# Replanning the DMA queues of a statically ordered attention and Fourier-MLP kernel

## The chip, the cores and the metric

The kernel runs on one core of one Trainium2 chip. The metric is the device time of one execution in microseconds (us); the time of a kernel is the median over its runs. Five engines work side by side on a core: TensorE (PE, with its weight loads as PEld), VectorE (DVE), ScalarE (ACT), GpSimd (POOL) and SyncE (SP). In this kernel DMA transfers are issued by two of them, SP and POOL, which makes two queues.

## The reference

Four batches, eight heads, 768 positions, head size 64; model width 512, MLP width 2048. All tensors are float32.

```python
P = sort_net                                   # (4, 8, 8, 8)
for _ in range(5):                             # Sinkhorn
    P = exp(P - max(P, -1)); P = P / sum(P, -1); P = P / sum(P, -2)
k_sorted = einsum('bhij,bhjcd->bhicd', P, k in 8 blocks of 96)   # v_sorted likewise
scores = 0.125 * q_block @ k_sorted_block.T    # 96 x 96, block by block
x = softmax(scores) @ v_sorted_block           # (4, 768, 512) over all heads
u = x + real(fft(fft(x, axis=1), axis=2))
un = (u - mean(u)) / sqrt(var(u) + 1e-6)
out = u + relu(un @ w_ch1) @ w_ch2
```

## The kernel before

The whole program is a list of steps, each with the engines that may do it, its cost in nanoseconds on each, and the buffers that it reads and writes. `Plan.run` puts the steps in order before anything runs: it keeps a clock for each engine, looks at all steps whose predecessors are placed, and places the one that can start first (among those within 40 ns, the one of highest priority). `Plan.emit` then advances the clocks. What it writes out is a fixed order of instructions for each engine; on the chip an engine takes its instructions in that order and waits at each for its operands. So a cost or a release time in the planner changes no instruction, but it changes where each one stands.

For DMA steps the planner before has two kinds of cost. Bulk loads have `kb`, and share one transfer clock at 0.235 KB per ns with 1800 ns of start. All other transfers have a fixed `hop` after the issue, raised by 1500 ns while that clock is ahead. `rel` is a time before which a step isn't placed. `need` gives a step a priority by due time.

The work of a batch, with the names of steps and lines that come up later:

- Loads. `load_v` (L432, SP, 384 KB each for a pair of heads), `load_kq` (L440, POOL, 192 KB each after the conversion to 16 bit), `weights` (L1097 for `w1`, L1101 for `w2`, POOL, four parts of 512 KB each), `load_const` (L1107, SP: `cse`, `cso`, `cdh`, `cdl`, `negm`, `lm`, `rsel`, `idx`).
- Block sorting. `make_kron` (L473) spreads the Sinkhorn matrix; `v_cast`, `v_sum` (POOL, L459 to L461); `q_mix` (L625), `k_mix` (L642) and its evictions to `kz`; `v_mix` (L596, L598), evicted into `vo`. `v_move` (L608) moves `vo` to the layout `vs`, in twelve transfers of 65 KB a batch; only in batch 0 may POOL issue some of them. `a_out` (L578) and `row_zero` (L586) are small moves of rows.
- Attention. In batches 0 and 1 each head has its maxima (L700, L703), scores again (L716, L719) and the exponential (L724). In batches 2 and 3 the step `turned` does it in the transposed layout: scores (L737), minima (L747), eight exponentials (L742), `es` (L757 or L759), and two DMA transposes `turn_e` on SP (L761) into `eT`. `values` is L783 with the division L789, L790.
- Fourier part. Folds (L807, L812), transforms along the sequence (`dft_s`, L828, L849) and along the width (`dft_d`, L881 to L897), `residual` (L924, L927), `add_res` (POOL, L947, L948), `store_u` (L954), statistics (L965), `normal` (L990, L993), and the transposes of the normed rows: on PE (L1016) or, in batches 2 and 3, mostly by DMA (`turn_u`, L1006).
- MLP. Two groups of 384 rows a batch: 64 matmuls L1044 with the relu L1050, then 48 matmuls L1065, the sum with `u` (L1072), loaded by `load_u` (L1030), and a scattered store on POOL (L1087). The planner puts MLP into gaps of the other work and at the end.

Batch b + 1 is loaded and mixed while batch b is in its attention and Fourier part.

Of the kernel before, what the change touches and what calls it, by code (L numbers as in the profile page):

```python
# [187 lines left out]
class Step:  # L188
    __slots__ = ("name", "b", "on", "fn", "pre", "data", "succ", "wait", "use", "kb", "hop", "prio", "fin", "by", "rel",
                 "extra")  # L190


class Plan:
    LAG, PE_TAIL, MARGIN, NEAR = 45.0, 215.0, 120.0, 40.0
    DMA_START, DMA_RATE, DMA_CROWD = 1800.0, 0.235, 1500

    def __init__(self, engines):
        self.engines, self.rings = engines, {}
        self.wrote, self.read = {}, {}
        self.todo = []  # L200
        self.free = dict.fromkeys(engines, 0.0)
        self.dma = 0.0
        self.began = False
# [5 lines left out]

    def step(self, name, b, on, fn, r=(), w=(), kb=0, hop=0, need=None, prio=None, rel=0.0):  # L210
        s = Step()
        s.name, s.b, s.on, s.fn, s.kb, s.hop, s.rel = name, b, on, fn, kb, hop, rel
# [69 lines left out]
    def start(self, free):  # L282
        for s in self.wrote.values():
            s.fin = free["T"]
        self.free = dict(free)
        self.dma = free["T"] + 1500
        for r in self.rings.values():
            for h in r.held:
                if h is not None:
                    h.free_at = free["T"]  # L290

    def run(self):
# [9 lines left out]
        while ready:  # L302
            found = []
            for s in ready:
# [26 lines left out]
def kernel(  # L331
# [96 lines left out]
    def load_v(b, hp, need):  # L428
        v32[b, hp] = Buf("hr" if 4 * b + hp in (0, 1, 2, 3, 7) else "v32")

        def f(e):
            nc.sync.dma_start(v_view(b, hp), v[b, 2 * hp:2 * hp + 2].rearrange(  # L432
                "h (p g) d -> p h (g d)", g=G))
        step("load_v", b, {"S": 400}, f, w=[v32[b, hp]], kb=393, need=need, rel=18000 if b == 1 else 0.0)

    def load_kq(b, hp, need):
        hs = slice(2 * hp, 2 * hp + 2)
        for d, src, tag in ((k16, k, "k16"), (q16, q, "q16")):
            d[b, hp] = Buf(tag)
            step("load_" + tag, b, {"G": 740}, lambda e, t=d[b, hp], src=src: nc.gpsimd.dma_start(  # L440
                t.t, src[b, hs].rearrange("h (p g) d -> p h (g d)", g=G)),
                w=[d[b, hp]], kb=393, need=need, rel=32000 if b == 1 else 0.0)

# [131 lines left out]
    def a_out(b):  # L575
        def f(e):
            for p, lo, hi, at in ((BLK, 0, 8, 0), (BLK + 1, 0, 7, 1), (BLK + 1, 7, 8, 4)):
                nc.sync.dma_start(xr2[b % 2][p:p + 1, lo:hi].rearrange("o i m -> o (i m)"),  # L578
                                  a16[at:at + hi - lo])
        step("a_out", b, {"S": 2100}, f, r=["a16"], w=[("xa", b % 2)], hop=4500)  # L580

    def row_zero(b):
        def f(e):
            xr = xr2[b % 2]
            for lo, hi, at in ((0, 7, 1), (7, 8, 4)):
                nc.sync.dma_start(xr[BLK + 2:BLK + 3, lo:hi], xr[0:1, at:at + hi - lo])  # L586
        step("row_zero", b, {"S": 1100}, f, r=[("x", b % 2, h, y) for h in range(H) for y in range(2)],
             w=[("x0", b % 2)], hop=4500)

# [15 lines left out]
    def v_move(b, half):  # L605
        for g in range(G):
            def f(e, g=g):
                (nc.gpsimd if e == "G" else nc.sync).dma_start(  # L608
                    vs[2 * (b % 2) + half][16 * g:16 * g + 16].rearrange("c i e -> c (i e)"),
                    vo[half][:, g].rearrange("p h e -> p (h e)"))  # L610
            step("v_move", b, {"S": 600, "G": 560} if b == 0 else {"S": 600}, f,
                 r=[("vo", 4 * half + j) for j in range(4)], w=[("vs", b % 2, half, g)], hop=5500)

    qT = {}

    def q_mix(b, hp):
# [14 lines left out]
        plan.chain(("psQ", b, {"T": 530}, f, [q16[b, hp]], [pQ]),  # L631
                   ("qT", b, {"A": 799, "V": 545}, ev, [pQ], [qT[b, hp]]))

    def k_mix(b, hp, gh):
# [11 lines left out]
        def ev(e, hh):  # L646
# [4 lines left out]
                 SCALE if b < TURN else -SCALE)  # L651
        plan.chain(("psK", b, {"T": 360}, f, [k16[b, hp], (kron[b], hp // 2)], [pK]),
                   *[("kz", b, {"A": 484, "V": 551}, lambda e, hh=hh: ev(e, hh), [pK],
# [74 lines left out]
    def turned(n):  # L728
# [22 lines left out]
        for y in range(2):  # L751
            es = Buf("es")

            def g(e, y=y, es=es):
# [196 lines left out]
    def store_u(b, i, m):  # L951
# [3 lines left out]
            u_dram[b][BLK * t:BLK * t + BLK], us[b, i, m].t[o:o + BLK]),  # L955
            r=[us[b, i, m]], w=[("ud", b, t)], hop=3300)

# [41 lines left out]
    def transpose_u(b, i, m):  # L999
# [5 lines left out]
        if b >= 2 and (i, m) != (0, 1):  # L1005
            step("turn_u", b, {"S": 1250}, lambda e: nc.sync.dma_start(  # L1006
                unT[b, t // 4].t[:, :, BLK * (t % 4):BLK * (t % 4) + BLK],
                un[b, i, m].t[0:BLK], transpose=True),
                r=[un[b, i, m]], w=[(unT[b, t // 4], t % 4)], hop=4000)
            return  # L1010
# [12 lines left out]
    def mlp(b, gr):  # L1023
        hr, ur = {}, {}

        def load_u(t):
# [4 lines left out]
                 r=[("ud", b, j) for j in range(8) if BLK * j < r1 and BLK * j + BLK > r0],  # L1031
                 w=[ur[t]], hop=2800, prio=MLP - 1e8)
        MLP = 1e6 + 1e4 * b
# [43 lines left out]
    def store(b, q_, o, prio):  # L1077
        if (b, q_) == (B - 1, 5):
            for y, (r, n, k0, st) in enumerate((
# [3 lines left out]
                step("store", b, {e_: 400}, lambda e, r=r, n=n, k0=k0, st=st: plan.engines[e].dma_start(  # L1083
                    out[b, k0:k0 + st * (n - 1) + 1:st], o.t[r:r + n]), r=[o], hop=2000, prio=prio)
            return
# [3 lines left out]
            out_offset=bass.IndirectOffsetOnAxis(ap=idx[:, c:c + 1], axis=0),  # L1089
            in_=o.t, in_offset=None), r=[o, "idx"], hop=2500, prio=prio)  # L1090

    def weights(i, need):
        c = i % 4

        def f(e):
# [4 lines left out]
            else:  # L1100
                nc.gpsimd.dma_start(  # L1101
                    w2sb[:, 4 * c:4 * c + 4],
                    moe_w_ch2[DM * c:DM * c + DM].rearrange("(c p) m -> p c m", p=128))
        step("weights", 0, {"G": 770}, f, w=[("w1" if i < 4 else "w2", c)], kb=1048, need=need, rel=45000)

    def load_const(key, need, t, d):
        step("const", 0, {"S": 400}, lambda e: nc.sync.dma_start(t, d.ap()),  # L1107
             w=[key], kb=int(np.prod(t.shape)) * 2 // 1000 + 1, need=need)

# [177 lines left out]
```

## Time and profile before

| | |
|---|---|
| median of three runs | 333.4 us (332.53 to 333.9) |
| profiled execution | 334.52 us |
| its span | 332.4 us |
| granted TensorE clock, mean | 0.979 |
| instructions | 7517 |
| PE busy | 301.2 us (91% of the span) |
| VectorE busy, ScalarE busy | 216.3 us, 213.6 us |
| GpSimd busy | 143.4 us |
| DMA moved | 45.75 MB, 138 GB/s on the mean |
| costliest line on PE | L1044, 512 matmuls, 91.5 us; L1065, 384 matmuls, 89.5 us |

The span runs from the first to the last instruction of the profiled execution; its own time is 2.1 us longer and 1.1 us above the median. A busy PE is modelled from pipelined matmuls, so groups of matmuls overlap by a little in the timeline. In the timeline a line gives start, length, engine, line, operation, operands and the number of instructions merged, and in brackets the idle time of the engine before it and what ended that.

### The profile page before, as it was taken

Reading aid. Unit: us, or ns where it says so; the run is one execution under the profiler, and the core shown is the slowest. Engines: PE = TensorE matmul, PEld = TensorE weight load, DVE = VectorE, ACT = ScalarE, POOL = GpSimd, SP = SyncE. Lnnn points to the kernel's source line nnn. Section 1 sums busy time; section 2 is a strip of 40 time slices with the busy share of each in tenths; the row PEclk is TensorE's granted clock in tenths of the full one; section 3 lists DMA queues with packets and bytes.
Section 4 is the critical chain, followed back from the end, with each engine's and each line's share of the span. In section 5 each row is a group of like instructions: output and inputs, shape, how many; then the busy total and the mean of one; then the engine's idle time right before and its main releaser. Section 6 shows DMA issues by size and latency. Waiting matters only on the chain.

```text
span 332.4 us, 7517 instructions
## 1 busy us (share of the span) xinstructions
PE 301.2 (91%) x2758; PEld 191.9 (58%) x2758; DVE 216.3 (65%) x482; ACT 213.6 (64%) x522; POOL 143.4 (43%) x199
## 2 busy tenths in 40 slices
PE   0998898978999989967999998999999999999993
PEld 0367875746876665545666764566565464554641
DVE  6678796889998999548997899965840502002010
ACT  5564886877798889866985767884276371440710
POOL 8885687778014997323201732310940511202111
PEclk9997998987999999999999999999999999999999
DMA  6999969999607769655425545631651613404112
GB/s 177 216 300 172 164 124 184 233 240 246 174 3 126 137 192 189 188 148 104 109 52 145 146 124 128 170 100 25 172 184 27 184 65 104 130 4 128 63 63 64
DMA packets 53868, 45.75 MB, mean 138 GB/s; under 512 B 23537, under 2 KB 45520, under 8 KB 53832
## 3 DMA queue, kind: packets, MB, share of 16 engines
q1 hardware_dynamic: 38840, 28.31, 32.2%
q0 software_dynamic: 14992, 16.97, 26.7%
q8 instruction: 21, 0.34, 0.5%
q14 instruction: 15, 0.12, 0.1%
HBM read 35.36 MB, written 12.58 MB: 144 GB/s over the span
## 4 chain that ended last, share of the span: by engine, by line
PE 45%; DVE 7%; ACT 5%; issue 3%; DMA 3%; SPq 1%; POOLq 0%; DVEq 0%; ACTq 0%
PE bank L1044 18%; PE bank L1065 18%; ACT sm L742 2%; PE bank L828 1%; DVE es L759 1%; PE bank L783 1%; DMA v<-in_v_dram 1%; DVE mns L747 1%; DVE st L965 1%; PE bank L897 1%; DMA out_dram<-outt,idx_sb 1%; PE bank L737 1%; ACT hr L1050 1%; DMA u_dram<-u 1%; PE bank L596 1%
## 5 line engine op out<-in xcount | busy, mean ns | idle before, releaser
L1044 PE MATMUL bank<-unT,w1sb 128*128 128x384 f16 x512 | 91.5, 329 | 2.4 <-DVE xr L790 2.2
L1065 PE MATMUL bank<-w2sb,hr 128*128 128x512 f16 x384 | 89.5, 379 | 0.1
L1050 ACT ACTIVATE hr<-bank 128x384 f16<-128x384 f32 x128 | 61.7, 492 | 39.5 <-PE bank L1044 38.4
L1044 PEld LDWEIGHTS <-w1sb 128*128 128x128 f16 x512 | 49.1, 99 | 33.5 <-issue 3.3
L1087 POOL DMA_INDIRECT out_dram<-outt,idx_sb x23 | 22.7, 987 | 87.5 <-DVE outt L1072 69.0
L1065 PEld LDWEIGHTS <-hr 128*128 128x128 f16 x384 | 36.5, 98 | 39.5
L1072 DVE SCALAR_TENSOR_TENSOR outt<-ur,bank 128x512 f32<-128x512 f32 x24 | 16.4, 682 | 60.4 <-PE bank L1065 58.0
L742 ACT ACTIVATE sm<-bank,mns 96x96 f32<-96x96 f32 x128 | 31.7, 354 | 6.5 <-DVE mns L747 6.4
L947 POOL TENSOR_TENSOR u<-u,P 96x257 f32<-96x257 f32 (+1 forms) x16 | 11.9, 741 | 39.9 <-issue 15.7
L459 POOL TENSOR_TENSOR v<-v 128x384 f32<-128x384 f32 x11 | 11.0, 1004 | 34.7 <-ACT v L413 22.9
L965 DVE BATCH_NORM_STATS2 st<-u 96x6 f32<-96x512 f32 (+1 forms) x32 | 21.8, 682 | 5.8 <-POOL u L948 5.5
L790 DVE TENSOR_TENSOR xr<-bank,rz 96x512 f16<-96x512 f32 x32 | 22.0, 687 | 1.1
L415 ACT ACTIVATE kz<-bank 64x384 f16<-64x384 f32 x40 | 18.5, 482 | 4.6 <-DVE kz L419 3.8
L783 PE MATMUL bank<-vs,eT 97*96 97x65 f16 x256 | 16.1, 208 | 1.3 <-DVE xr L790 0.5
L807 DVE TENSOR_TENSOR xs<-xr 96x512 f16<-96x512 f16 x32 | 16.9, 540 | 0.3
L783 PEld LDWEIGHTS <-eT 97*96 97x96 f16 x256 | 15.0, 125 | 3.5 <-issue 1.9
L413 ACT COPY u<-bank 96x512 f32<-96x512 f32 (+1 forms) x19 | 10.8, 583 | 8.2 <-issue 3.8
L828 PE MATMUL bank<-cso_sb,xs 96*128 96x384 f16 x64 | 13.1, 326 | 3.2 <-DVE xs L807 3.1
L419 DVE TENSOR_SCALAR kz<-bank 64x384 f16<-64x384 f32 x24 | 12.9, 556 | 4.3 <-ACT kz L415 3.5
L413 ACT CAST W<-bank 128x384 f16<-128x384 f32 (+1 forms) x38 | 12.9, 378 | 4.0 <-PE bank L828 2.5
L993 DVE TENSOR_SCALAR un<-u,mv,rstd 96x512 f16<-96x512 f32 (+1 forms) x19 | 12.0, 641 | 5.1 <-PE bank L1016 5.1
L440 POOL DMA_DIRECT2D k<-in_k_dram x16 | 11.9, 747 | 7.7 <-PE bank L642 5.0
(142 smaller groups left out, 574.6 us busy)
## 6 DMA issues: line engine op xcount, KB each, us to landing
u_dram<-u SPq DMA_DIRECT2D x32, 192.0 KB
ur<-u_dram SPq DMA_DIRECT2D x24, 256.0 KB
v<-in_v_dram SPq DMA_DIRECT2D x11, 384.0 KB
k<-in_k_dram POOLq DMA_DIRECT2D x16, 192.0 KB, 5.7
q<-in_q_dram POOLq DMA_DIRECT2D x16, 192.0 KB, 5.2
vs<-vo SPq DMA_DIRECT2D x42, 65.0 KB
w1sb<-in_moe_w_ch_dram POOLq DMA_DIRECT2D x4, 512.0 KB, 11.2
w2sb<-in_moe_w_ch_dram POOLq DMA_DIRECT2D x4, 512.0 KB, 19.1
```

Source lines behind the costliest of these rows:

```text
L413: nc.scalar.copy(dst, src)
L415: nc.scalar.activation(dst, src, AF.Copy, scale=scale)
L742: nc.scalar.activation(sm.t[:, i], pair(pS, BLK)[:, y, i % 4], AF.Exp, bias=mn.t[:, i:i + 1], scale=-1.0)
L783: nc.tensor.matmul(ps[:, i // 4, i % 4], eT[n].t[0:97, i, :], vs[2 * (b % 2) + h // 4][:, i, (D + 1) * (h % 4):(D + 1) * (h % 4 + 1)])
L790: nc.vector.tensor_tensor(xr2[b % 2][0:BLK, :, D * h:D * (h + 1)].rearrange("p (t j) d -> p t j d", t=2), ps[:, :, :, 0:D], r[:, :, :, Non ...
L807: nc.vector.tensor_tensor(xs[b, hp, par].t, xr[0:BLK, 0:4, ms], xr[0:BLK, 4:8, ms], op=ALU.subtract if par else ALU.add)
L828: nc.tensor.matmul(ps, xs[b, hp, 1].t[:, j, :], cso[:, j, :], start=(j == 0), stop=(j == 3))
L965: nc.vector.bn_stats(st.t[0:n], us[b, i, m].t[0:n])
L1044: nc.tensor.matmul(ps, w1sb[:, mc, 128 * fc:128 * fc + 128], unT[b, gr].t[:, mc, :], start=(mc == 0), stop=(mc == 3))
L1050: nc.scalar.activation(dst, bank(pH, [128, 384]), AF.Relu)
L1065: nc.tensor.matmul(ps, hr[f4].t[:, fc % 4, 128 * t:128 * (t + 1)], w2sb[:, fc, :], start=(fc == 0), stop=(fc == 15))
L1087: step("store", b, {"G": 1020}, lambda e: nc.gpsimd.indirect_dma_start(out=out.rearrange("b s m -> (b s) m"), out_offset=bass.IndirectOffs ...
```

## The change

No operation is added or taken away: the edits are in the planner's account of DMA and in the numbers of the DMA steps.

- `kb` gives way to `work` (time that the transfer takes in its queue), `hop` (time from there to landing), `lanes` (how many of the eight transfers in flight it takes) and `bulk`.
- Each of the two queues, SP and POOL, has a clock of its own. A transfer that starts while the other queue is busy lengthens both, and lands up to 2400 ns later.
- A queue has eight transfers in flight: the ninth is placed when the first has landed.
- A bulk transfer is placed only when the busier queue is less than 800 ns ahead.
- `v_move` may be issued by POOL in every batch, not in batch 0 alone.
- Release times: values of the second batch at 27 us (were 18), its q and k at 29 (were 32), `w1` at 41 and `w2` at 78 (both were 45), inputs of the third batch at 80; `cdh`, `cdl` at 22, `lm`, `rsel`, `idx` at 27 (all had none).
- Planned times: DMA transposes 1250 + 600 + 600 ns (were 1250 + 4000), moves 600 + 450 + 1500 (were 600 + 5500), stores of `u` 350 + 500 + 1300 (were 350 + 3300), loads of `u` 430 + 800 + 2000 (were 430 + 2800); on PE `q_mix` 445 (was 530) and `k_mix` 255 (was 360).

The core of the diff:

```diff
 class Plan:
-    DMA_START, DMA_RATE, DMA_CROWD = 1800.0, 0.235, 1500
+    DMA_AHEAD = 800
...
-        self.dma = 0.0
+        self.dma = {"S": 0.0, "G": 0.0}
+        self.lanes = {"S": [0.0] * 8, "G": [0.0] * 8}
...
-            tail[s] = min(s.on.values()) + (3000.0 if s.kb else s.hop) + max(
+            tail[s] = min(s.on.values()) + (s.work + s.hop + 500.0 if s.hop else 0.0) + max(
...
-        if s.kb:
-            self.dma = max(self.dma, done) + s.kb / self.DMA_RATE
-            done = self.dma + self.DMA_START
         if s.hop:
-            done += s.hop + (self.DMA_CROWD if self.dma > done else 0.0)
+            other = "G" if e == "S" else "S"
+            begin = max(done, self.dma[e])
+            ahead = max(0.0, self.dma[other] - begin)
+            shared = min(s.work, ahead)
+            self.dma[e] = begin + s.work + shared
+            self.dma[other] += shared
+            done = self.dma[e] + s.hop + min(2400.0, ahead)
+            self.lanes[e] = self.lanes[e][s.lanes:] + [done] * s.lanes
...
-                        t = max([at] + [p.fin for p in s.pre if p.by != e or p.kb or p.hop])
+                        t = max([at] + [p.fin for p in s.pre if p.by != e or p.hop])
+                        if s.hop:
+                            t = max(t, self.lanes[e][s.lanes - 1])
+                            if s.bulk:
+                                t = max(t, max(self.dma.values()) - self.DMA_AHEAD)
...
-        step("load_v", b, {"S": 400}, f, w=[v32[b, hp]], kb=393, need=need, rel=18000 if b == 1 else 0.0)
+        step("load_v", b, {"S": 400}, f, w=[v32[b, hp]], work=1250, hop=1450, bulk=True, need=need, rel=80000 if b == 2 else 27000 if b == 1 else 0.0)
...
-                w=[d[b, hp]], kb=393, need=need, rel=32000 if b == 1 else 0.0)
+                w=[d[b, hp]], work=1200, hop=1500, bulk=True, need=need, rel=80000 if b == 2 else 29000 if b == 1 else 0.0)
...
-            step("v_move", b, {"S": 600, "G": 560} if b == 0 else {"S": 600}, f,
-                 r=[("vo", 4 * half + j) for j in range(4)], w=[("vs", b % 2, half, g)], hop=5500)
+            step("v_move", b, {"S": 600, "G": 560}, f,
+                 r=[("vo", 4 * half + j) for j in range(4)], w=[("vs", b % 2, half, g)], work=450, hop=1500)
...
-                r=[es], w=[(et, y)], hop=4000)
+                r=[es], w=[(et, y)], work=600, hop=600)
...
-        step("weights", 0, {"G": 770}, f, w=[("w1" if i < 4 else "w2", c)], kb=1048, need=need, rel=45000)
+        step("weights", 0, {"G": 770}, f, w=[("w1" if i < 4 else "w2", c)], work=3000, hop=1500, bulk=True, need=need, rel=41000 if i < 4 else 78000)
```

The built programs show what the planner makes of it. Both have the same 5261 rows on PE, in another order. Of the twelve moves of a batch, SP issues 6, 6, 5 and 4 (batches 0 to 3; before 6, 12, 12 and 12), POOL the others. On POOL the four loads of `w1` stand apart between value sums and adds, and the four of `w2` behind the adds of batch 0; before, all eight stood in a row. On SP, the values of batch 1 and `lm` come behind the moves of batch 0; before, ahead of them. On PE, the first three pairs' k_mix comes ahead of batch 0's v_mix and the fourth right behind it. VectorE has 492 instructions (482 before) and ScalarE 512 (522).

More of the change, by code (lines that the diff above doesn't have):

```diff
@@ L188 @@
 class Step:
-    __slots__ = ("name", "b", "on", "fn", "pre", "data", "succ", "wait", "use", "kb", "hop", "prio", "fin", "by", "rel",
+    __slots__ = ("name", "b", "on", "fn", "pre", "data", "succ", "wait", "use", "work", "hop", "lanes", "bulk", "prio", "fin", "by", "rel",
                  "extra")
@@ L208, in buf, with step @@
         return b
[L210 removed]
+    def step(self, name, b, on, fn, r=(), w=(), work=0, hop=0, lanes=1, bulk=False, need=None, prio=None,
+             rel=0.0):
         s = Step()
[L212 removed]
+        s.name, s.b, s.on, s.fn, s.work, s.hop, s.rel = name, b, on, fn, work, hop, rel
+        s.lanes, s.bulk = lanes, bulk
         s.data, s.pre, s.succ, s.fin, s.by, s.extra = set(), set(), set(), None, None, []
@@ L285, in start @@
         self.free = dict(free)
-        self.dma = free["T"] + 1500
+        self.dma = dict.fromkeys("SG", 16000)
+        self.lanes = {e: [15000] * 8 for e in "SG"}
         for r in self.rings.values():
@@ L579, in f @@
                                   a16[at:at + hi - lo])
-        step("a_out", b, {"S": 2100}, f, r=["a16"], w=[("xa", b % 2)], hop=4500)
+        step("a_out", b, {"S": 2100}, f, r=["a16"], w=[("xa", b % 2)], work=150, hop=1500, lanes=3)
     def row_zero(b):
@@ L587, in row_zero @@
         step("row_zero", b, {"S": 1100}, f, r=[("x", b % 2, h, y) for h in range(H) for y in range(2)],
-             w=[("x0", b % 2)], hop=4500)
+             w=[("x0", b % 2)], work=100, hop=1100, lanes=2)
     def v_mix(b, h):
@@ L630, in ev @@
                  bank(pQ, [128, G, 128], F16).rearrange("x g (i c) -> x i g c", c=16))
-        plan.chain(("psQ", b, {"T": 530}, f, [q16[b, hp]], [pQ]),
+        plan.chain(("psQ", b, {"T": 445}, f, [q16[b, hp]], [pQ]),
                    ("qT", b, {"A": 799, "V": 545}, ev, [pQ], [qT[b, hp]]))
@@ L651, in ev @@
                  SCALE if b < TURN else -SCALE)
-        plan.chain(("psK", b, {"T": 360}, f, [k16[b, hp], (kron[b], hp // 2)], [pK]),
+        plan.chain(("psK", b, {"T": 255}, f, [k16[b, hp], (kron[b], hp // 2)], [pK]),
                    *[("kz", b, {"A": 484, "V": 551}, lambda e, hh=hh: ev(e, hh), [pK],
@@ L955, in store_u @@
             u_dram[b][BLK * t:BLK * t + BLK], us[b, i, m].t[o:o + BLK]),
-            r=[us[b, i, m]], w=[("ud", b, t)], hop=3300)
+            r=[us[b, i, m]], w=[("ud", b, t)], work=500, hop=1300)
     def stats(b, i):
@@ L1008, in transpose_u @@
                 un[b, i, m].t[0:BLK], transpose=True),
-                r=[un[b, i, m]], w=[(unT[b, t // 4], t % 4)], hop=4000)
+                r=[un[b, i, m]], w=[(unT[b, t // 4], t % 4)], work=600, hop=600)
             return
@@ L1031, in load_u @@
                  r=[("ud", b, j) for j in range(8) if BLK * j < r1 and BLK * j + BLK > r0],
-                 w=[ur[t]], hop=2800, prio=MLP - 1e8)
+                 w=[ur[t]], work=800, hop=2000, prio=MLP - 1e8)
         MLP = 1e6 + 1e4 * b
@@ L1083, in store @@
                 step("store", b, {e_: 400}, lambda e, r=r, n=n, k0=k0, st=st: plan.engines[e].dma_start(
-                    out[b, k0:k0 + st * (n - 1) + 1:st], o.t[r:r + n]), r=[o], hop=2000, prio=prio)
+                    out[b, k0:k0 + st * (n - 1) + 1:st], o.t[r:r + n]), r=[o], work=300, hop=1300, prio=prio)
             return
@@ L1089, in store @@
             out_offset=bass.IndirectOffsetOnAxis(ap=idx[:, c:c + 1], axis=0),
-            in_=o.t, in_offset=None), r=[o, "idx"], hop=2500, prio=prio)
+            in_=o.t, in_offset=None), r=[o, "idx"], work=800, hop=1400, prio=prio)
     def weights(i, need):
@@ L1103, in f @@
                     moe_w_ch2[DM * c:DM * c + DM].rearrange("(c p) m -> p c m", p=128))
-        step("weights", 0, {"G": 770}, f, w=[("w1" if i < 4 else "w2", c)], kb=1048, need=need, rel=45000)
+        step("weights", 0, {"G": 770}, f, w=[("w1" if i < 4 else "w2", c)], work=3000, hop=1500, bulk=True, need=need, rel=41000 if i < 4 else 78000)
     def load_const(key, need, t, d):
         step("const", 0, {"S": 400}, lambda e: nc.sync.dma_start(t, d.ap()),
-             w=[key], kb=int(np.prod(t.shape)) * 2 // 1000 + 1, need=need)
+             w=[key], work=6 * int(np.prod(t.shape)) // 1000 + 50, hop=1500, bulk=t.shape[-1] > 1, need=need,
+             rel=27000 if key in ("lm", "rsel", "idx") else 22000 if key in ("cdh", "cdl") else 0.0)
     rst = const.tile([32, NB], F32, name="rst")
```

## The prediction

> **What bounds the kernel now.** I read the page first, then the busy time by stretches, then TensorE's and VectorE's idle times in the timeline, then the DMA issues. The page's rows of share, clock and DMA:
>
> ```profile
> PE 301.2 (91%) x2758; PEld 191.9 (58%) x2758; DVE 216.3 (65%) x482; ACT 213.6 (64%) x522; POOL 143.4 (43%) x199
> ...
> PEclk9997998987999999999999999999999999999999
> DMA  6999969999607769655425545631651613404112
> ```
>
> PE is busy for 301.2 of 332.4 us. Its first matmul waits 9.08 us for the Sinkhorn steps (L542), its last one ends at 326.9, so 5.5 us of tail follow, and 332.4 - 301.2 - 9.1 - 5.5 = 16.6 us is idle time between matmuls. From 264.6 us on the chain is MLP matmuls alone, back to back (L1044, L1065). PE's work is the same in both kernels, so the change can earn only from these 16.6 us and from a better clock, and can lose wherever PE, which takes its instructions in order, meets a later operand. By stretches of 10 us the idle time lies so: 0.3 in 10 to 20, 6.05 in 20 to 80, 2.4 in 80 to 140, 5.65 in 140 to 160, 2.2 in 160 to 220, 0.3 in 310 to 320 and 0 in between. The four stretches that count, after the column heads:
>
> ```profile
> core 0: us, PE busy (x) PEld busy (x) DVE busy (x) ACT busy (x) POOL busy (x), PEclk, DMA share, GB/s
> 20.00:30.00 10.00, 8.55 (x124) 6.56 (x125) 9.39 (x16) 5.11 (x12) 6.60 (x10) 0.90 1.11 260
> 70.00:80.00 10.00, 8.52 (x69) 5.29 (x67) 9.38 (x18) 6.72 (x16) 8.99 (x13) 0.66 1.21 242
> 140.00:150.00 10.00, 6.84 (x72) 4.68 (x72) 3.38 (x9) 6.73 (x19) 3.13 (x5) 1.00 0.57 148
> 150.00:160.00 10.00, 7.51 (x88) 5.02 (x83) 9.11 (x20) 7.53 (x24) 3.86 (x6) 1.00 0.49 93
> ```
>
> In the first two the DMA share is above 1 and VectorE is nearly full; in 140 to 150 both PE and VectorE starve while DMA is half idle. The timeline there shows why:
>
> ```profile
> 135.62 5.05 SPq L608 DMA_DIRECT2D vs<-vo  x8
> ...
> 142.04 4.87 SPq L761 DMA_TRANSPOSE eT<-es  x2
> ...
> 147.62 0.36 DVE L759 TENSOR_SCALAR es<-sm 96x384 f16<-96x384 f32 x1 [2.51 <-DMA eT<-es]
> ...
> 148.37 0.82 PE L828 MATMUL bank<-cso_sb,xs 96*128 96x384 f16 x4 [2.30 <-DVE xs L807]
> ...
> 150.50 0.56 DVE L417 CAST v<-v 128x768 f16<-128x768 f32 x1 [2.19 <-DMA v<-in_v_dram]
> ```
>
> SP issues the twelve moves of batch 2 (L608) from 132.97 to 141.95, and the transposes and batch 3's value loads stand behind them. VectorE waits 2.51 us for a transpose and 2.19 for a load, and PE waits for VectorE (2.30 us here, 2.15 at 152.81 for L790). The DMA issues and the start:
>
> ```profile
> q<-in_q_dram POOLq DMA_DIRECT2D x16, 192.0 KB, 5.2
> ...
> w1sb<-in_moe_w_ch_dram POOLq DMA_DIRECT2D x4, 512.0 KB, 11.2
> w2sb<-in_moe_w_ch_dram POOLq DMA_DIRECT2D x4, 512.0 KB, 19.1
> ```
> ```profile
> 18.29 0.73 POOL L440 DMA_DIRECT2D q<-in_q_dram  x1
> ...
> 28.87 0.85 PE L625 MATMUL bank<-ident,q 128*64 128x128 f16 x12
> 29.39 0.73 POOL L440 DMA_DIRECT2D k<-in_k_dram  x1 [2.69 <-DMA q<-in_q_dram]
> ...
> 40.87 0.52 PE L700 MATMUL bank<-kz,qT 128*96 128x96 f16 x8 [0.88 <-ACT kz L415]
> ```
>
> The load of q for heads 6 and 7 takes 10.5 us (18.29 to 28.82), since SP queued 2.7 MB of constants and values ahead of it from 14.26 on; the matching k lands at 31.9.
>
> **The sum, part by part.** The span is 332.4, the profiled execution 334.5, the median of the three runs 333.4; the terms are differences on the profile's time and are taken from the median.
>
> *Front, 18 to 45 us.* In the new order `cdh`, `cdl` are behind the short `a_out`, and `lm` and all values of batch 1 behind batch 0's moves; only `cse`, `cso`, `negm` (0.43 MB) are ahead of that q. Loads with little beside them land in 3.4 to 4.3 us (L440 at 108.35 and 105.55), so q is there at about 23 and k, issued when L642 frees its buffer, at about 25. PE's order uses this: all four head pairs' k_mix stands ahead of the scores, where now the fourth (L642) comes at 37.98. Of the 2.3 us of gaps in 20 to 45 I take 1.7 away: the 0.88 at 40.87 wholly, over half of the rest, in which VectorE's maxima bind. Ends: -2.3, and +1.5 as three more kz evictions (0.49 to 0.56 each) get ahead of the first maxima. **-1.7.**
>
> *Weights, 46 to 88 us.* All eight loads leave POOL at 46.2 to 51.4 and occupy the rings until 77.2. Behind them a move takes 6.3 to 8.6 us from issue to landing, against 2.4 to 2.6 at 172 to 177, and as a ninth issue on SP waits until the first of eight has landed (the issue at 72.09 follows a landing at 72.08), the stores and moves stretch from 65 to 83. PE's share of that is the 2.4 us of gaps in 70 to 90, such as 0.56 at 74.86 behind an eviction that waited 0.94 for `u_dram<-u`. The new POOL order has the four w1 loads apart, between sums and adds, and w2 after batch 0's adds, near 80 us. Cover: w1's last part lands at 63.2 now and L1044 starts at 75.5; w2 at 80 + 4 x 3.3 (the pace of L1097) + 5 lands at 98, and L1065 starts at 112.3. I take half of the gaps: **-1.2** (ends -2.4 and 0).
>
> *Moves on two queues.* Now batch 0 has six on each and batches 1 to 3 twelve on SP; then 6, 5 and 4 stay on SP and 6, 7 and 8 go to POOL. An SP issue is 0.59 us on the mean, so for batch 2 SP is free 7 x 0.59 = 4.1 us sooner, which is as much as the two PE gaps of 4.45 us. But one transpose took 3.57 us to issue (142.04) where 1.2 is usual; these 2.37 us were no queue of moves, and I leave them in. 4.45 - 2.37 = **-2.1** (ends -5.65 and 0). On POOL, seven issues of 0.56 stand ahead of value sums and of the loads of k for heads 4 to 7, which the new order puts behind them: 7 x 0.56 + two sums of 1.94 + 0.75 + 4.3 to land = 12.9 us, beside 11.8 us of matmuls between the last L598 of batch 2 and that k_mix. **+0.5** (0 to 1.6).
>
> The Trainium skill, "DMA: Bandwidth & Descriptors", section "Issuing engines are not separate DMA queues", says that a second issuing engine saves the issue time alone, which is usually small beside the transfer. Here it isn't small: 0.59 us of issue each, one after another, against 2.4 to 2.6 us of landing that overlap. By the rule taken strictly the moves would give nothing, and the sum would be 2.1 us worse.
>
> *Tighter plan.* `turn_e` and `turn_u` were planned at 1250 + 4000 ns, now 1250 + 600 + 600. From the semaphore updates of the trace, the 32 transposes of L761 land 2.2 to 6.3 us after issue, median 3.0, mean 3.25; 22 of 32 are later than 2.45 us, 2 later than 5.25. So the reserve that took up lateness is gone. In PE's order the work between a head's scores (L737) and its values (L783) is 12.4 us at the least now; in the new one five of the 16 heads have 8.8 to 10.9. The head's own chain is 0.5 + 0.94 (L747) + 2.0 (eight exponentials) + 0.5 (es) + two issues of 1.2 + 2.3 to land, about 8.6 us. Queued behind a late L783 is all of PE, MLP too. Five heads x 0.8 us (3.25 - 2.45), a third of it met by nothing else: **+1.3** (0 to 16 x 0.8 = 12.8).
>
> *Nothing for the rest.* Ten evictions more go to VectorE and ten fewer to ScalarE; VectorE is at 9.5 to 9.8 of 10 from 80 to 100 and 110 to 130, but PE has MLP to do there (within 1 us). The last groups are as they were: batch 3 is through before MLP needs it in both orders.
>
> Sum: -1.7 - 1.2 - 2.1 + 0.5 + 1.3 = -3.2, so 333.4 - 3.2 = **330.2 us**; the case's own range is 327 to 333.
>
> **Rivals.**
>
> *Tight plan loses (slower).* Place: L783 of batches 2 and 3, 125 to 220 us. Each late transpose holds PE, and the next head's buffers with it. For it: the median is above the planned 2.45. Against it: half of the present lateness stands beside the crowding that goes. Gains of 5.0 less 0.5 are used up when 4.5 of 12.8 us, 35%, is exposed; at 70% it is 333.4 - 4.5 + 9.0 = 337.9 us.
>
> *Hidden anyway (no change).* VectorE, not the queues, sets the pace to 130 us, and the 142 us stall recurs. Then only part of the moves' gain is left: 333.0.
>
> *The clock (faster still).* The granted clock is 0.50 in 28.1 to 31.5, 55.4 to 58.8 and 72.5 to 79.3, with 13.0 us of PE work in it; at full clock that is 6.5 less, of which some 3.4 (the first two, where VectorE isn't full) reach the end: 330.2 - 3.4 = 326.8. The 3.41 us before each had PE busy for only 2.41, 2.57 and 2.15, and the change fills that stage. Against it: 144 to 154 us has 1.92, 2.29 and 1.57 and kept 1.00. The Trainium skill, "TensorE: Matmul & The Clock Gate", section "What's actually happening", ties the half clock to an idle window and full clock to a busy one of some 3.4 us; the trace has the window's length, but not so plain a rule.
>
> That the edit does nothing can be left out: the order of the built program has the moves and weights where it says.
>
> **How the numbers follow.** Forecast 0.48, tight plan 0.25, hidden 0.17, clock 0.10. A measurement here tells about 0.5% (1.7 us; the three runs spread by 1.4). Below 331.7 lie 0.43 of the forecast's chance, the clock's 0.10 and 0.02 of hidden: 0.55. Above 335.1: the tight plan's 0.25 and 0.02 of hidden: 0.27; 0.18 between. The range 325 to 338 leaves out a tenth above and a few hundredths below.
>
> **What would show it.** Right: the load of q at 18 us lands within 5 us; no w2 transfer before 75 us, moves of batch 1 landing in under 4; SP's moves of batch 2 take about 3 us; PE idle in 20 to 90 below 5 us, in 140 to 160 below 3.5. Wrong: PE waiting on L783 or for VectorE behind L783 by more than 4 us in 125 to 220; a wait of L642 for k near 140 us; L1065 waiting for w2.

## The result, and the profile after

| | before | after |
|---|---|---|
| median | 333.2 us (332.5 to 333.9, four runs) | 344.6 us (339.9 to 350.0, four runs) |
| ratio to before | 1 | 1.0284, 95% interval 1.0206 to 1.0362 |
| profiled execution, its span | 334.5 us, 332.4 us | 342.9 us, 340.9 us |
| PE: busy, end of the last matmul | 301.2 us, 326.9 us | 305.3 us, 335.1 us |
| idle between PE's matmuls | 16.6 us | 20.7 us |

By the medians the kernel became 11.4 us slower, where 330.2 us was forecast. Here and below a ratio goes by the faster runs of a kernel alone (two of the four after, 346.3 and 350.0 us, are left out), so that it says 9.5 us where the medians say 11.4. Lines of the changed kernel are 12 higher than before (13 from `weights` on): L761 is L773, L783 is L795, L608 is L620. The page's rows of share, clock and DMA:

```profile
PE 305.3 (90%) x2758; PEld 193.6 (57%) x2758; DVE 220.5 (65%) x492; ACT 211.7 (62%) x513; POOL 154.3 (45%) x219
...
PEclk9999789978999999989999999999999999999998
DMA  7959898997954699993978443641371521503212
```

The busy time in the four stretches that were shown of before, with 130 to 140 and 160 to 170 added:

```profile
core 0: us, PE busy (x) PEld busy (x) DVE busy (x) ACT busy (x) POOL busy (x), PEclk, DMA share, GB/s
20.00:30.00 10.00, 8.96 (x148) 6.53 (x143) 9.94 (x19) 6.39 (x15) 5.15 (x9) 1.00 0.86 178
70.00:80.00 10.00, 8.47 (x71) 6.00 (x71) 8.80 (x19) 6.36 (x13) 8.09 (x12) 0.66 0.77 196
130.00:140.00 10.00, 7.10 (x61) 4.17 (x60) 7.41 (x17) 7.00 (x21) 6.88 (x12) 1.00 1.07 138
140.00:150.00 10.00, 7.75 (x56) 4.64 (x54) 5.25 (x15) 2.95 (x7) 4.96 (x8) 0.83 1.24 200
150.00:160.00 10.00, 9.99 (x134) 6.22 (x132) 9.01 (x20) 8.90 (x25) 3.77 (x6) 1.00 0.25 34
160.00:170.00 10.00, 7.27 (x88) 4.76 (x86) 9.22 (x17) 5.85 (x21) 4.80 (x7) 1.00 1.02 163
```

PE is idle for 1.04 us in 20 to 30 (1.45 before), but over 20 to 45 for as long as before (2.63 and 2.61). The stall of 150 to 160 is gone, 2.25 of 3.16 us are left in 140 to 150, and new gaps stand at 120 to 140 (4.3 us in place of 0.5) and from 160 on. Summed, PE's idle time went from 7.0 to 5.8 us in 20 to 90, from 1.0 to 0.3 in 90 to 120, from 6.2 to 6.6 in 120 to 160, and from 2.2 to 7.7 in 160 to 230. The timeline of the changed kernel at two of these gaps:

```profile
134.89 1.22 SPq L773 DMA_TRANSPOSE eT<-es  x1
...
142.67 0.37 PE L795 MATMUL bank<-vs,eT 97*96 97x65 f16 x4 [2.25 <-DMA eT<-es]
...
168.96 0.52 ACT L769 ACTIVATE es<-sm 96x384 f16<-96x384 f32 x1 [1.49 <-DMA eT<-es]
...
171.60 0.37 PE L795 MATMUL bank<-vs,eT 97*96 97x65 f16 x4 [1.05 <-DMA eT<-es]
171.65 0.36 DVE L771 TENSOR_SCALAR es<-sm 96x384 f16<-96x384 f32 x1 [2.14 <-DMA eT<-es]
```

The transpose issued at 134.89 stands among twelve moves on both queues and lands 7.74 us later; PE has been waiting for it for 2.25. ScalarE and VectorE wait too, since `es`, the source of a transpose, has three buffers. POOL, which the lines below leave out, waits 2.0 us for one. The chain of waits has "DMA eT<-es 5%"; the lines that it names of before have no transpose. The waits that transposes ended in the changed kernel:

```profile
PE bank L795 <- DMA eT<-es: 3.9, 3, 2.3
...
ACT es L769 <- DMA eT<-es: 3.0, 3, 1.5
...
DVE es L771 <- DMA eT<-es: 2.1, 1, 2.1
```

(total, times, longest). Before, PE had none, and the other two 1.9 and 3.3.

### The profile page after: what moved, and what is told of

It is laid out like the page before. It is cut to its first block, busy times and chain, and to the rows that moved or that the text cites. A ratio compares the mean times of both kernels' runs of the same rounds, so it can differ in the third digit from the quotient of the medians.

```text
span 340.9 us, 7526 instructions
## 1 busy us (share of the span) xinstructions
PE 305.3 (90%) x2758; PEld 193.6 (57%) x2758; DVE 220.5 (65%) x492; ACT 211.7 (62%) x513; POOL 154.3 (45%) x219
## 4 chain that ended last, share of the span: by engine, by line
PE 37%; DMA 8%; DVE 8%; ACT 4%; issue 2%; SPq 1%; POOL 0%; POOLq 0%; ACTq 0%; DVEq 0%
PE bank L1056 18%; PE bank L1077 14%; DMA eT<-es 5%; ACT sm L754 2%; DMA ur<-u_dram 1%; DVE st L977 1%; DVE es L771 1%; DVE outt L1084 1%; DVE xr L802 1%; PE bank L909 1%; DVE un L1005 1%; DMA out_dram<-outt,idx_sb 1%; DVE kz L431 1%; DMA xr<-xr 1%; PE bank L795 1%
## 5 line engine op out<-in xcount | busy, mean ns | idle before, releaser
L1077 PE MATMUL bank<-w2sb,hr 128*128 128x512 f16 x384 | 89.5, 379 | 0.5 <-DVE outt L1084 0.4
L1056 PEld LDWEIGHTS <-w1sb 128*128 128x128 f16 x512 | 50.0, 100 | 33.5 <-issue 3.5
L1077 PEld LDWEIGHTS <-hr 128*128 128x128 f16 x384 | 36.4, 98 | 39.7 <-issue 0.8
L1084 DVE SCALAR_TENSOR_TENSOR outt<-ur,bank 128x512 f32<-128x512 f32 x24 | 16.4, 684 | 46.1 <-PE bank L1077 43.9
L1005 DVE TENSOR_SCALAR un<-u,mv,rstd 96x512 f16<-96x512 f32 (+1 forms) x21 | 13.9, 661 | 26.7 <-DMA unT<-un 18.3
L620 POOL DMA_DIRECT2D vs<-vo x27 | 14.5, 545 | 18.4 <-issue 9.0
L795 PE MATMUL bank<-vs,eT 97*96 97x65 f16 x256 | 16.5, 212 | 5.7 <-DMA eT<-es 3.9
L427 ACT ACTIVATE kz<-bank 64x384 f16<-64x384 f32 x36 | 16.9, 486 | 5.4 <-DVE kz L431 4.0
L795 PEld LDWEIGHTS <-eT 97*96 97x96 f16 x256 | 15.3, 129 | 7.9 <-DMA eT<-es 4.3
L425 ACT COPY u<-bank 96x512 f32<-96x512 f32 (+1 forms) x26 | 14.7, 585 | 6.3 <-PE bank L936 4.1
L736 ACT ACTIVATE sm<-bank 96x768 f32<-96x768 f32 x16 | 12.6, 804 | 7.3 <-PE bank L731 6.9
L425 ACT CAST W<-bank 128x384 f16<-128x384 f32 (+1 forms) x39 | 13.6, 393 | 5.5 <-PE bank L840 3.1
L1002 ACT ACTIVATE un<-u,nm,rstd 96x512 f16<-96x512 f32 (+1 forms) x11 | 8.9, 813 | 11.7 <-DMA unT<-un 9.1
L431 DVE TENSOR_SCALAR kz<-bank 64x384 f16<-64x384 f32 x28 | 14.9, 549 | 2.0 <-PE bank L654 1.2
```

Source lines behind the costliest of these rows:

```text
L425: nc.scalar.copy(dst, src)
L431: nc.vector.tensor_scalar(dst, src, scale, None, op0=ALU.mult)
L795: nc.tensor.matmul(ps[:, i // 4, i % 4], eT[n].t[0:97, i, :], vs[2 * (b % 2) + h // 4][:, i, (D + 1) * (h % 4):(D + 1) * (h % 4 + 1)])
L1005: nc.vector.tensor_scalar(o, x, scalar1=mv[b, i].t[0:n, m, 0:1], scalar2=rstd[b, i].t[0:n, m:m + 1], op0=ALU.subtract, op1=ALU.mult)
L1056: nc.tensor.matmul(ps, w1sb[:, mc, 128 * fc:128 * fc + 128], unT[b, gr].t[:, mc, :], start=(mc == 0), stop=(mc == 3))
L1077: nc.tensor.matmul(ps, hr[f4].t[:, fc % 4, 128 * t:128 * (t + 1)], w2sb[:, fc, :], start=(fc == 0), stop=(fc == 15))
```

## The experiments

The theories at the start. T2: transposes planned to land after 2.45 us instead of 5.25 put their readers too close behind them; this planned time, from the start of the issue to the landing, is called the lead below. T1: the order has a hole, as the loads of k for the third batch's head pairs 3 and 4 stand on POOL behind the moves, their key mixing comes at 151 us (before at 108 and 120), and two batches of attention are squeezed into what is left. T3: the moves slow each other on two queues, and the transposes between them. Each run is compared by its ratio to the kernel before, run beside it on the same chip; bracketed pairs are 95% intervals.

**e1_lead.** The changed kernel with the old lead of the transposes:

```diff
# turn_e, and turn_u alike
-                r=[es], w=[(et, y)], work=600, hop=600)
+                r=[es], w=[(et, y)], work=600, hop=3400)
```


> The changed kernel with one part undone: the DMA transposes are planned at 5250 ns from the start of the issue to landing again (1250 + 600 + 3400) instead of 2450. The planner then also puts the key mixing of the third batch's head pairs 3 and 4 (L654 of the changed kernel) ahead of the moves, not 26 us behind them. Theory T1 (the hole: the loads of k for these pairs stand on POOL behind the moves, their scores come 26 us late, and the attention of two batches is squeezed into 150 to 230 us beside loads): about 337 us, gaps of PE in 120 to 230 us down from 14.3 to about 9. Theory T2 (late transposes because of the short lead alone): about 337 us too, but with the waits for eT<-es gone (3.9 us now). Theory T3 (two queues slow each other's moves and the transposes between them): 343 us, no change against the changed kernel.

Measured: 332.6 us, 0.9939 [0.9884, 0.9993]. All of the loss is gone: the ratios differ by 0.0345 of 333 us, 11.5 us, with about 3.2 either way. No engine waits for a transpose any more, and the idle time of PE in 120 to 230 us is 7.0 instead of 14.3. The hole closed too (key mixing of pairs 3 and 4 at 110 and 111 us), so this run alone doesn't tell T1 from T2.

**e2_inputs, e3_moves_sp, e4_no_pacing.** The changed kernel with another part undone, the short lead kept:

```diff
# e2: inputs of the third batch (values, and q and k alike)
-                rel=80000 if b == 2 else 27000 if b == 1 else 0.0)
+                rel=27000 if b == 1 else 0.0)
# e3
-            step("v_move", b, {"S": 600, "G": 560}, f,
+            step("v_move", b, {"S": 600, "G": 560} if b == 0 else {"S": 600}, f,
# e4
-    DMA_AHEAD = 800
+    DMA_AHEAD = 1e9
```


> The changed kernel with one part undone: the inputs of the third batch may be loaded before 80 us again (the release time of 80000 is gone for q, k and v; the second half of the weights keeps its 78 us). Planned order: key mixing of pairs 3 and 4 about half way between the two kernels. T1: about 340 us, half of the hole's price back. T2: 343 us, and more waits for eT<-es than now, since values stand closer behind scores. T3: 343 us.

> The changed kernel with one part undone: the moves of batches two to four are planned and issued on SP alone, as in the kernel before. Planned order: key mixing of pairs 3 and 4 behind the moves still, by about 24 us of matmul work where the kernel before has 17 and the changed one 36. T1: about 341 us. T2: 343 us, no change. T3: about 338 us, moves land in 2.6 us again instead of 5, transposes between them in 3.5 instead of 4.8.

> The changed kernel with one part undone: bulk loads are no longer held back until the busier queue is less than 800 ns ahead. Planned order: key mixing of pairs 3 and 4 stands ahead of the moves, as in the kernel before, and the four parts of w2 and the loads of k and q come in a row. T1: about 337 us. T2: 343 us. T3: 343 us or more, since the loads crowd the moves.

Measured: e2 352.9 us, 1.0595 [1.0515, 1.0675]; e3 347.2 us, 1.0431 [1.0334, 1.0529]; e4 339.2 us, 1.0199 [1.0130, 1.0267]. None of them gets back to before. In e4 the hole is closed (109 and 121 us) and PE is idle for only 2.2 us in 120 to 160, yet for 8.8 in 160 to 230. Its time lies nearer to the 337 us of T1 than to the 343 of T2, and what it gains on the changed kernel (0.0085, with 0.0104 either way) is not clear of noise; but with the hole closed and the lead short it is still 0.0260 slower than e1, 8.7 us with 2.9 either way (pacing differs as well). That speaks against T1 as the main cause. e3 has its moves landing in 3.4 us (median) instead of 5.0 and is no faster: against T3. The waits for `eT<-es` on PE, ScalarE and VectorE together are 9.0 us in the changed kernel, 21.5 in e2, 16.4 in e3, 9.7 in e4 and 0 in e1. e2 and e3 were expected at 343 us by T2 and came out slower. That a short lead makes one pay at once for whatever brings readers nearer or crowds the transposes is argued from this, not shown.

**e5_before_short, e6_lead_u, e7_lead3250, e8_lead7250.** The lead alone: shortened in the kernel before; given back to `turn_u` alone; two other sizes.

```diff
# e5, in the kernel before, turn_e and turn_u
-                r=[es], w=[(et, y)], hop=4000)
+                r=[es], w=[(et, y)], hop=1200)
# e7 (e8: hop=5400), in the changed kernel, turn_e and turn_u; e6: hop=3400 for turn_u alone
-                r=[es], w=[(et, y)], work=600, hop=600)
+                r=[es], w=[(et, y)], work=600, hop=1400)
```


> The kernel before with one part of the change alone: both DMA transposes planned at 2450 ns from the start of the issue to landing (1250 + 1200) instead of 5250; all else as before. T2 (the short lead): waits for eT<-es over PE, ScalarE and VectorE rise from 5.2 us to 9 or more, and the time is 339 to 345 us. Rival T4 (the short lead only hurts together with the new queue costs, pacing and release times): 333 us, within 1%.

> The changed kernel with the lead of 5250 ns given back to turn_u (the transposes of the normed rows) alone; turn_e stays at 2450. T2 in the form that the head's transposes turn_e carry the price: 343 to 346 us, as the changed kernel. If turn_u carries it: about 333 us.

> The changed kernel with both transposes planned at 3250 ns, the mean of the landings measured in the kernel before. If a mean is what a plan needs: 333 us, as with 5250. If the price is the sum of the single latenesses beyond the plan (in the changed kernel 39.9 us beyond 2.45, 24.8 beyond 3.25, 6.0 beyond 5.25, where 12 us came back between the first and the last): about 332.6 + 12.0 x (24.8 - 6.0) / (39.9 - 6.0) = 339 us.

> The changed kernel with both transposes planned at 7250 ns, past nearly all landings. By the lateness that is left beyond 5.25 (0.7 us in the run with 5250) nothing more is to be gained: 332 to 333 us; if distance costs (buffers held longer, values later), 334 to 336 us. Waits for eT<-es stay near 0.

Measured: e5 341.4 us, 1.0272 [1.0225, 1.0318]; e6 346.4 us, 1.0423 [1.0327, 1.0519]; e7 339.0 us, 1.0171 [1.0105, 1.0237]; e8 333.2 us, 1.0008 [0.9969, 1.0047]. e5 settles it: one number in the kernel before, with no other part of the change and no hole in the order (key mixing of pairs 3 and 4 at 110 and 125 us), costs 9 us; T4 falls. e6 puts the price on the heads' transposes, `turn_e`. Under the new account of DMA the hole comes with the short lead (in e6 at 148 us) and goes with the long one (e1, e8), so the 11.5 us hold the hole's price too. By the 8.7 of e4 and the 9.1 of e5 that is up to some 3 us, which lies within the intervals. e7 shows that a mean is not enough: planned at 3.25 us, near the 3.37 of its own landings, it is still about 7 us behind e1. The sum of single latenesses beyond the plan gave 339, and 339.0 came, but so close a hit is luck: the interval is 2.2 us either way, and e4, with 69.4 us of lateness beyond 2.45 in its own trace where the changed kernel has 39.9, is the faster of the two. Past 5.25 us no more is to be had (e8).

**e9_lead_sp, e10_before_two.** The two queues by themselves, with the order on every engine kept; only who issues a move is changed:

```diff
# e9, on top of e1
-                (nc.gpsimd if e == "G" else nc.sync).dma_start(
+                (nc.gpsimd if e == "G" and b == 0 else nc.sync).dma_start(
# e10, in the kernel before
-                (nc.gpsimd if e == "G" else nc.sync).dma_start(
+                (nc.gpsimd if e == "G" or b > 0 and g % 2 else nc.sync).dma_start(
```


> The run with 5250 ns of lead, its order on every engine kept as it is, but each move of batches two to four that stands on POOL is issued by SP at the same place of the order. If two queues are worth the 2.1 us that the prediction gave them: 0.994 + 0.006 = 1.000 of the time of before (about 334.5 us against 332.5). If the second queue only lets the moves slow each other (landing 5.2 us on two queues, 2.6 on one): 0.994 or less.

> The kernel before, its order on every engine kept, but every second move of batches two to four is issued by POOL at the same place of the order. By the prediction's term: 2.1 us faster than before (0.994). If issue time was not what held PE at 140 to 160 us, or if moves on two queues land later: 1.000, with moves of the third batch landing in about 5 us instead of 2.6.

Measured: e9 335.5 us, 1.0046 [1.0000, 1.0092]; e10 339.6 us, 1.0194 [1.0135, 1.0253]. Against e1, taking the second queue away costs 0.0107, or 3.6 us, with about 2.4 either way. It is not lost where the prediction had it: PE's idle time in 120 to 160 is 4.3 us in e9 and 4.7 in e1, while e9 has 2.5 us more in 20 to 120 and 1.5 more in 160 to 230. e10 was expected at 0.994 or 1.000 and is slower, and its timeline says why:

```profile
75.25 0.56 POOL L608 DMA_DIRECT2D vs<-vo  x1 [3.19 <-DMA w2sb<-in_moe_w_ch_dram]
...
79.94 0.73 POOL L440 DMA_DIRECT2D k<-in_k_dram  x1 [4.14 <-DMA w2sb<-in_moe_w_ch_dram]
...
82.14 0.69 DVE L965 BATCH_NORM_STATS2 st<-u 96x6 f32<-96x512 f32 x1 [10.42 <-POOL u L948]
...
85.87 0.80 PE L716 MATMUL bank<-nident_sb,mxs 96*96 96x96 f16 x8 [11.27 <-DVE mxs L703]
```

In the kernel before, the eight loads of weights fill POOL's queue at this place. The moves of the second batch put on it wait for a part of `w2` to land, POOL's adds (L947, L948) wait behind them, VectorE for the adds, and PE stands for 11.27 us. At 120 to 160 us the same edit does what the prediction said: PE is idle there for 2.8 us instead of 6.2. The second queue pays only if the weights are out of its way.

**e11_lead_w2, e12_lead_front.** Two more parts undone on top of e1:

```diff
# e11
-        ... rel=41000 if i < 4 else 78000)
+        ... rel=41000)
# e12: constants; values of the second batch; its q and k
-             rel=27000 if key in ("lm", "rsel", "idx") else 22000 if key in ("cdh", "cdl") else 0.0)
+             rel=0.0)
-                ... rel=80000 if b == 2 else 27000 if b == 1 else 0.0)
+                ... rel=80000 if b == 2 else 18000 if b == 1 else 0.0)
-                ... rel=80000 if b == 2 else 29000 if b == 1 else 0.0)
+                ... rel=80000 if b == 2 else 32000 if b == 1 else 0.0)
```


> The run with 5250 ns of lead, but w2 may be loaded from 41 us as w1, not from 78. By the prediction's term for the weights (1.2 us): 0.994 + 0.004 = 0.998 of before, idle time of PE in 70 to 90 us up again. If pacing and not the release time spreads the loads: 0.994. A re-planned order differs elsewhere too, so that 0.005 either way tells nothing.

> The run with 5250 ns of lead, but with the release times of the constants (cdh, cdl, lm, rsel, idx) taken away and those of the second batch's inputs as before (18 us for values, 32 for q and k). By the prediction's term for the front (1.7 us): 0.994 + 0.005 = 0.999 of before, and the loads of q and k at 18 to 30 us land in 8 to 10 us again. If pacing alone keeps them apart: 0.994, loads landing in about 5.

Measured: e11 333.7 us, 1.0037 [0.9999, 1.0075]; e12 330.2 us, 0.9894 [0.9821, 0.9967]. `w2` at 78 us is worth 0.0098 here, 3.3 us, as far as a re-planned order tells. But PE's idle time in 70 to 90 was not its place: there it is 1.2 us in e11 and 1.8 in e1. The release times of the front are worth nothing; without them the kernel is the fastest so far. The fourth load of q, which took 10.5 us before, lands in 5.5 us in e12 without them, so the rest of the new account keeps the early loads apart.

**e13_four_es, e14_other_leads.** What was left open on the price of the lead: its way to the end, and whether the other shortened transfers have a share.

```diff
# e13, in the changed kernel: es is taken in turn from four buffers, the plan goes by three
-    ring("es", 3, [BLK, 4, 128], F16)
+    ring("es", 3, [BLK, 4, 128], F16)
+    es_more = [const.tile([BLK, 4, 128], F16, name=f"es_more{i}") for i in range(1)]
+    plan.rings["es"].cycle = plan.rings["es"].tiles + es_more
# e14, in the changed kernel: moves hop=5050 (was 1500), a_out 4350 (1500), row_zero 4400 (1100), store_u 2800 (1300)
```


> The changed kernel, its order on every engine kept, with a fourth buffer for es (the source of the transposes), used in turn, so that ScalarE and VectorE wait less for a transpose to be through before they write the next es (3.0 and 2.1 us in the changed kernel). If the lateness reaches the end through these waits: 340 us or less. If it reaches it through PE's own waits at the values (3.9 us) and what is queued behind them: 343 to 345 us.

> The changed kernel with the planned times of the other small transfers as in the kernel before (moves 600 + 5500, a_out and row_zero + 4500, stores of u + 3300), and the transposes still at 2450. If the transposes alone carry the price: 341 to 346 us. If any reserve in the plan does as well: about 334 us.

Measured: e13 343.0 us, 1.0186 [1.0113, 1.0258]; e14 344.8 us, 1.0339 [1.0284, 1.0393]. With four buffers ScalarE and VectorE no longer wait for a transpose, PE's own waits are 5.1 us, and the ratio comes down by 0.0098, with 0.0106 either way. So most of the price goes another way, through PE's waits at the values by T2; up to some 3 us through the other two engines can't be ruled out. The reserve of the other transfers replaces nothing.

**e15_front_lead6250, e16_front_again, e17_front_short.** The kernel of e12 with a lead of 6250 ns (`hop=4400`), as it was, and with the short lead of the change (`hop=600`):

> The run without the release times of the front (lead 5250), with the lead at 6250. No theory asks for a gain: 0.99 of before, within 0.006; tried as the fastest version.

> The same kernel as the run without the release times of the front (lead 5250), on another occasion: 0.989 of before, within 0.006, if it is faster than before; 0.995 to 1.000 if that was chance.

> The run without the release times of the front, with the transposes planned at 2450 again: a third pair that differs in the lead alone. By the other two pairs (+12 us in the changed kernel, +9.3 in the kernel before): 339 to 344 us.

Measured: e15 334.7 us, 1.0005 [0.9951, 1.0058], so a longer lead gains nothing; e16 327.0 us, 0.9883 [0.9820, 0.9947]; e17 341.8 us, 1.0249 [1.0158, 1.0341]. e12 and e16 are one kernel, and both occasions have it about 1.1% faster than before and 4% faster than the changed kernel. e16 and e17 ran on one chip and differ in the lead alone, by 14.8 us (12.2 by the ratios); e17 has the hole too (key mixing of pairs 3 and 4 at 133 and 137 us, in e16 at 105.5 and 107.1). The timeline of e17 shows a long wait for a transpose:

```profile
156.14 10.96 SPq L773 DMA_TRANSPOSE eT<-es  x4
156.35 1.44 POOL L452 DMA_DIRECT2D q<-in_q_dram  x2
...
157.77 1.46 POOL L452 DMA_DIRECT2D k<-in_k_dram  x2
...
165.34 0.53 PE L795 MATMUL bank<-vs,eT 97*96 97x65 f16 x4 [4.14 <-DMA eT<-es]
...
167.81 0.53 PE L795 MATMUL bank<-vs,eT 97*96 97x65 f16 x4 [1.93 <-DMA eT<-es]
```

Three transposes issued beside four loads of q and k (384 KB of source each) land 9.16, 9.50 and 8.28 us after their issue, where the plan said 2.45; PE stands for 4.14 and 1.93 us, and a half clock with 4.6 us of PE's work in it follows from 165.0 on. The two kernels in 160 to 230 us, e17 and then e16:

```profile
160.00:230.00 70.00, 58.33 (x510) 37.62 (x508) 50.82 (x118) 45.68 (x138) 21.57 (x31) 0.93 0.58 113
```
```profile
160.00:230.00 70.00, 67.68 (x582) 42.98 (x581) 61.48 (x141) 52.44 (x161) 29.64 (x43) 1.00 0.52 115
```

Three pairs differ in the lead alone. Idle time is PE's between its matmuls; the clock's loss is half of PE's busy time at a granted clock of 0.5; all from the profiled executions, in us:

| | span | idle 20 to 160 | idle 160 to 230 | clock's loss | waits for eT: PE | ScalarE and VectorE |
|---|---|---|---|---|---|---|
| before | 332.4 | 14.1 | 2.2 | 6.5 | 0 | 5.2 |
| e5, short | 339.3 | 15.6 | 3.3 | 8.2 | 3.1 | 7.4 |
| e1 | 331.3 | 12.0 | 2.3 | 8.4 | 0 | 0 |
| after, short | 340.9 | 12.6 | 7.7 | 8.5 | 3.9 | 5.1 |
| e16 | 323.5 | 9.3 | 2.3 | 1.7 | 0 | 0.3 |
| e17, short | 339.9 | 10.4 | 11.7 | 7.3 | 6.9 | 11.2 |

From e16 to e17 the two columns of idle time give 10.5 us and the clock 5.6, together 16.1 of the 16.4 us between the spans. From e1 to after idle time gives 6.0 of 9.6, and PE is busy 3.7 us longer at about the same loss to the clock; what that is stays open. From before to e5 idle time gives 2.6 and the clock 1.7 of 6.9; the rest, busy time again, stays open too. PE's waits for `eT` are two thirds of the idle time added in the pairs e16, e17 and e1, after (6.9 of 10.5, 3.9 of 6.0), and in the third pair more than all of it (3.1 and 2.6); that the rest stands behind results of VectorE and ScalarE that come later in turn is argued from the order, not shown by a run. Nor does a run have the order of the short lead with its landings on time, so what that order costs by itself is not told apart from the late landings.

## Why the prediction was wrong

*Tighter plan, +1.3: the step that failed.* Mechanism, lines and place were named, as a term and as a rival; the size was off by nine. Measured 11.5 us from e1 to after (3.2 either way, and up to some 3 of it the hole's, which the working didn't have), against ends of 0 and 12.8. Three errors are in the working. First, "five heads x 0.8 us" took the mean landing less the plan. An early landing then pays for a late one, and it shouldn't: the positive parts alone are to be added. From the same trace of before, 22 of 32 transposes are late by 26.6 us together against 2.45, and by 1.3 us against 5.25. A third of 26.6 is 8.9 us, near what e5 measured on this kernel (9.1), but with the third a guess that is luck. Second, the landings were taken as given: against 2.45 us they are 39.9 us late in all in the changed kernel and 27.7 in e1, which differs in the lead alone. In e5, whose order has no hole, they are 24.4 late, no more than before, so the added lateness is not the short plan's alone; that it comes from the crowding behind the hole is argued, not tested. Third, "a third of it met by nothing else" was a guess, and only five heads were counted because the others stood far apart in PE's order. That distance was itself laid out by the short plan. The rival, at 35% exposure or more, had its point of decision right and its chance of 0.25 too low: 11.5 of 12.8 is 90%. What no run settles is how late landings become lost time beyond PE's own waits: e4 has more lateness and less loss.

*Front, -1.7.* The load of q at 18.19 us lands in 3.40 us (10.5 before), as forecast, but the gain isn't there: idle time in 20 to 45 is 2.63 us, as before, in 20 to 90 5.8, not below 5, and the release times behind it, taken away, made e1 0.005 faster on each of two occasions (within the intervals). The load was not what held PE for long.

*Weights, -1.2.* Right in sign, 3.3 us by e11, though the median landing of `w1` and `w2` (7.5 and 8.9 us, 11.2 and 19.1 before) didn't bring the moves of the second batch under 4 us: they land in 6.1 (7.8 before). No wait of L1077 for `w2` appeared. Part of its worth is shown by e10: weights in a row and moves on the same queue cost 11.27 us in one place.

*Moves on two queues, -2.1.* Right in sign and near in size: 3.6 us by e9, about 2.4 either way, though e9 doesn't lose it at the third batch's moves, the place forecast. SP's issues of the third batch's moves spread over 4.6 us instead of 9, and the idle time of 140 to 160 fell from 5.65 to 2.3 us, below the forecast 3.5; in the changed kernel 130 to 140 took 2.9 in its place. The Trainium skill's rule in "DMA: Bandwidth & Descriptors", section "Issuing engines are not separate DMA queues", holds in that only issue time is saved: with both queues in use the moves land in 5.2 us (median of e1), with SP alone in 3.2 (e9). Its "usually small" does not hold here: the wait is for twelve issues of 0.6 us, one after another, with transposes behind them.

*POOL's load of k behind the moves, +0.5.* It happened (issues at 141.5 and 142.2 us), and took the form of the order's hole, not of a wait of L654. What it costs by itself was not measured.

*The clock.* The rival expected a better clock. The changed kernel lost 8.5 us to it (before 6.5); e16 lost 1.7, which is half of its gain in span over before. By the Trainium skill, "TensorE: Matmul & The Clock Gate", section "What's actually happening", an idle window of about 3.4 us brings the half clock and a busy one ends it; the runs show a softer rule (last section).

With the lead at its old size the other parts together are worth 0.006 of the time, 2 us, where the forecast without its term for the plan had 4.5. The terms measured singly (3.6 and 3.3 us gained, some 1.7 lost by the front's release times) sum to about 5; the difference is within their intervals.

## What to carry to other kernels

A planned duration in a statically ordered kernel is a reserve as much as an estimate. Size it by the late landings of the trace, not by their mean: list max(0, landing - plan) for each, and take a plan that few pass. The sum of these is no price list, as e4 shows. Here the mean (3.25 us) cost about 7 us, and 5.25, which 2 of 32 landings passed, cost nothing that a longer plan gave back. When several parts are changed at once, undo the cheapest number first: three other parts undone on top of the short lead misled, two by making the kernel slower still.

## What the runs showed of the hardware

The half clock follows partly idle windows, not only idle ones. Cutting the 19 profiles, from 14 us to PE's last matmul, into windows of 3.41 us in step with the clock's records, at full clock: with PE busy below 1.2 us the next window was at half clock in 17 of 17; 1.2 to 2.0 us in 30 of 46; 2.0 to 2.8 in 13 of 151; above 2.8 in none of 1419. A busy window does not always end it either: after a window at half clock with PE busy for over 3.2 us, the next was still at half in 22 of 77; e8 stayed at half for 17.1 us with PE busy for 16.9. So a late operand that leaves PE idle for half of such a window is likely to be charged again: 3.4 us at half clock is 1.7 us of lost work.

A transpose of a head's half lands 2.2 to 2.4 us after its issue with little beside it (2.37 at 165.92 us in e17), and 8.3 to 9.5 us beside four loads that the other queue issued within 2.1 us (e17).
